# mLSTM with a bilinear feed-forward on one core: the weights' low words folded into the shifted high word, and the low part by one subtraction

## The chip, the cores and the metric

The kernel runs on one core of one Trainium2 chip. The core has a matrix engine (TensorE, PE in the profile, with its weight loads as PEld), a vector engine (VectorE, DVE), a scalar engine (ScalarE, ACT), GpSimd (POOL) and a queue engine that issues the DMAs (SyncE, SP). The metric is the time of one execution in device microseconds; lower is better.

## The reference

The inputs are q, k, v and an output gate (4 batches, 8 heads, 768 steps, 40 elements), an input and a forget gate per head and step, and three weight matrices. The first part is an mLSTM, written as a recurrence:

```
m_new = max(f[t] + m, i[t])
C = exp(f[t] + m - m_new) * C + exp(i[t] - m_new) * v[t] k[t]^T
n = exp(f[t] + m - m_new) * n + exp(i[t] - m_new) * k[t]
y[t] = sigmoid(o[t]) * (C q[t]) / max(|n . q[t]|, 1)
```

The second part takes y as x, 3072 tokens by 320, and computes `((x @ w_a) * (x @ w_b)) @ w_out` with w_a and w_b of 320 by 1536 and w_out of 1536 by 320. The weights are 64-bit floating-point numbers: the reference multiplies random numbers by a NumPy double and so gets doubles. The result is 32-bit.

## The kernel before

The recurrence is done in chunks of 128 steps: 6 chunks for each of 4 batches, 24 pieces of work, in the order of time and then of batch. A chunk is an attention inside the chunk (scores, decay factors, weighted sum) plus a product with the state C that the chunks before left. The feed-forward runs over nine blocks of two or three chunks (256 or 384 tokens); block kb is interleaved by hand with the attention of later chunks, by a counter in the outer loop (lines 912 to 928). For each of the 12 slices of 128 columns of w_a and w_b, `up` (line 685) makes two accumulators in PSUM, tag "pu" with three buffers; their product is split into a high and a low part, and `down` (line 664), two slices later, multiplies both with w_out into "pd".

Every operand of these products is held as two numbers of the reduced type fp32r, a high part h and a low part l with h + l close to the 32-bit value, and a product is made of three matmuls: h times h, h times l, l times h.

So the weights must first be turned from 64-bit words into an h and an l. That is `weights()`, lines 308 to 384. The weights come in 32 stages (`weight_stages`, line 276): per slice of 384 columns of w_a and w_b four stages of 128 rows, one stage with the 64 rows left of both, and three stages of 128 rows of w_out with 320 columns. `fetch(x)` issues the DMA of a stage's raw words on SP, four stages ahead. `first(x)` takes the words apart:

- L336, ScalarE: the high words, read as 32-bit numbers, are scaled by a Prelu into t, which lies in one of four shared tiles `step`. This makes the exponent fit.
- L343, VectorE: W is t's bits shifted left by three. W is the weight cut off to a 32-bit number, with the last three bits empty.
- L344, VectorE: t becomes W's sign and exponent bits alone.
- L346, VectorE: r is the low word as a whole number times 2^-52 times t, that is, what W lacks.

W and r take a buffer each of the pool tag "cv", which has eight. `second(x)`, called after `first(x + 1)`, makes the two parts:

- L359, ScalarE: h is W rounded to fp32r.
- L361 and L362, TensorE: two matmuls with the identity `eye[0]` and its negative `eye[1]` add r and -h in a PSUM tile pc, which takes one of the three "pu" buffers.
- L363, VectorE: l is pc + W.

h and l lie in the same memory as the raw words (tag s{x}), so L359 can't write before the last reader of the raw words is done. In the four stages with the 64 rows left, h and l go to tiles ct and then by four DMAs (L367, L368) to their place. The generator `weights()` is advanced by hand: at set points in the first attention chunks, and then every sixth step of the feed-forward. `need(x)` (line 303) advances it further where a matmul comes to use a stage. `issue_after` in these lines keeps an instruction behind a named one on its engine; apart from that the framework's scheduler sets the order of each engine's instructions, by priorities, from a simulation at compile time. It also places all waits and buffers.

The two identities of fp32r are made at the start from `ident` by two scalings on ScalarE (L65 to L67).

Of the kernel before, what the change touches and what calls it, by code (L numbers as in the profile page):

```python
# [8 lines left out]
F32 = mybir.dt.float32  # L9
BF16 = mybir.dt.bfloat16  # L10
F32R = mybir.dt.float32r
# [4 lines left out]
ALU = mybir.AluOpType  # L16
# [4 lines left out]
def kernel(  # L21
# [13 lines left out]
    nc = tc.nc  # L35
    B, H, S, D = q.shape
    DM, DFF = w_a.shape
    P = 128
# [5 lines left out]
    NTB = TB * P  # L44
    WCH = 384
    CVB = 8
# [6 lines left out]
    wpool = ctx.enter_context(tc.tile_pool(name="wpool", bufs=1))  # L53
# [4 lines left out]
    ps_up = ctx.enter_context(tc.tile_pool(name="ps_up", bufs=3, space=PSUM))  # L58
# [3 lines left out]

    ident = wpool.tile([P, P], F32, name="ident")
    make_identity(nc, ident)
    eye = [wpool.tile([P, P], F32R, name=f"eye{j}") for j in range(2)]  # L65
    for j in range(2):
        nc.scalar.mul(eye[j], ident, 1.0 - 2.0 * j)  # L67
    NQ = 2

    qk = [wpool.tile([P, 2, H, 64], F32, name=f"qk{j}") for j in range(NQ)]  # L70
# [20 lines left out]
    for j in range(3):  # L91
        r = slice(j * BH, (j + 1) * BH)
# [10 lines left out]
    x = ident[0:BH, 0:BH].rearrange("k (x j) -> k x j", j=2)  # L103
# [204 lines left out]
    def weights():  # L308
        stages = list(weight_stages())
        held = {}  # L310

        def fetch(x):
            if x < len(stages):
                src = stages[x]
                n = src[0].shape[1]
                raw = rpool.tile([P, n], I64, tag=f"s{x}", name=f"raw{x}")
                r0 = 0
                behind = [y for first, y in BEHIND if x >= first][-1]
                with tc.issue_after(issued[behind]), tc.issue_after(issued.get("w", issued[behind])):
                    for a in src:  # L320
                        raw_in = nc.sync.dma_start(raw[r0:r0 + a.shape[0]], a).ins
                        r0 += a.shape[0]
                issued["w"] = raw_in
                held[x] = [raw, n]

        def first(x):
            raw, n = held[x]
            W = cpool.tile([P, WCH], F32, tag="cv", name="cw", bufs=CVB)[:, :n]
            t = step[x % len(step)][:, :n]
            words = raw.bitcast(U32).rearrange("p (n w) -> p n w", w=2)  # L330
            lo, hi = words[:, :, 0], words[:, :, 1]
            wu, tu = W.bitcast(U32), t.bitcast(U32)


            with tc.issue_after(after["e", 0] if x > 2 else issued["k", 0]):
                nc.scalar.activation(  # L336
                    t, hi.bitcast(F32), AF.Prelu, scale=2.0 ** -112, alpha=-(2.0 ** 32)
                )

            step_of = (None, ("b", 0), ("b", 0), ("r", 0), ("r", 0))  # L340
            y = after[step_of[x] if x < len(step_of) and step_of[x] else ("r", 1)] if x > 0 else issued["k", 0]
            with tc.issue_after(y):
                nc.vector.tensor_scalar(wu, tu, 3, None, op0=ALU.logical_shift_left)  # L343
            nc.vector.tensor_scalar(tu, wu, 0xFF800000, None, op0=ALU.bitwise_and)  # L344
            r = cpool.tile([P, WCH], F32R, tag="cv", name="cr", bufs=CVB)[:, :n]
            nc.vector.scalar_tensor_tensor(r, lo, 2.0 ** -52, t, op0=ALU.mult, op1=ALU.mult)  # L346
            held[x] += [W, r]

        def second(x):

            ready[0] = x + 1
            raw, n, W, r = held.pop(x)
            w = ws[x] = rpool.tile([P, 2, n], F32R, tag=f"s{x}", name=f"w{x}")
            h, l = w[:, 0], w[:, 1]
            last = len(stages[x]) > 1
            if last:
                h, l = (cpool.tile([P, WCH], F32R, tag="ct", name="ct", bufs=2) for _ in range(2))
            with tc.issue_after(after["e", 0]):
                nc.scalar.copy(h, W)  # L359
            pc = ps_up.tile([P, NTB], F32, tag="pu", name=f"pc{x}")[:, :n]  # L360
            nc.tensor.matmul(pc, eye[0], r, start=True, stop=False)  # L361
            nc.tensor.matmul(pc, eye[1], h, start=False, stop=True)  # L362
            nc.vector.tensor_tensor(l, pc, W, op=ALU.add)  # L363
            if last:
                for j in range(2):
                    rows, other = (slice(64 * i, 64 * i + 64) for i in (j, 1 - j))
                    nc.sync.dma_start(w[rows, j].bitcast(F32), h[rows].bitcast(F32))  # L367
                    nc.sync.dma_start(w[other, j].bitcast(F32), l[rows].bitcast(F32))  # L368

        fetch(0)  # L370
        yield -1
        for x in range(1, 4):
            fetch(x)
        for x in range(len(stages) + 1):
            fetch(x + 4)
            if x < len(stages):
                first(x)
                yield x
            if x > 0:
                second(x - 1)  # L380
                yield x
        for x in qks2:
            for w in range(2):
                nc.gpsimd.memset(x[:, w, :, 3 * D:], 0.0)
# [527 lines left out]
    for kb in range(NB):  # L912
# [5 lines left out]
        for x, _ in enumerate(moe_block(kb)):  # L918
# [3 lines left out]
            while acc >= 1.0 and not done:  # L922
                acc -= 1.0
                r = next(att, ("done", 99))
# [34 lines left out]
```

## Time and profile before

| | |
|---|---|
| runs, median | 569.38 us (3 runs, 569.38 to 571.58) |
| profiled execution, span from first to last instruction | 572.6 us |
| TensorE matmuls | 551.1 us busy (96%), 4864 |
| VectorE | 429.3 us busy (75%), 992 |
| ScalarE | 215.4 us busy (38%), 526 |
| GpSimd | 130.2 us busy (23%), 182 |
| mean granted TensorE clock | 0.966 |
| data moved | 68.35 MB, 119 GB/s |

The profile is of one execution. Busy time of an engine counts the time in which at least one of its instructions runs. A matmul's end is modelled and matmuls overlap, so a group of matmuls has more busy time than it adds to the chain. The chain is followed back from the last instruction: at each step to whatever released it, or to the instruction before it on its engine. The granted clock is the share of full speed that TensorE was given. A row of a group has the line, engine, operation, out<-in by the program's names, shapes and count, then busy time and mean duration in ns, then the idle time of the engine before them and what ended it. No time of the profiled execution is given beside its span.

### The profile page before, as it was taken

What the parts mean: (1) busy time and instruction counts of PE and PEld (TensorE: products, weight loads), DVE (VectorE), ACT (ScalarE), POOL (GpSimd) and SP (SyncE); (2) the same over time, 40 slices, a digit from 0 to 9 for tenths busy, and PEclk for the clock granted to TensorE, in tenths of its full rate; (3) what the DMA queues carried; (4) which work ended last, traced back from release to release, by engine and by line L of the source; (5) the groups of instructions that cost most, each with busy time, mean ns of one, the idle gap of its engine ahead of it and who ended that gap; (6) DMA issues with size and microseconds to landing.
All of it is one profiled execution on the core that took longest, in us unless ns stands there. A gap on an engine that the chain in (4) does not pass through costs nothing.

```text
span 572.6 us, 12629 instructions
## 1 busy us (share of the span) xinstructions
PE 551.1 (96%) x4864; PEld 529.6 (92%) x4864; DVE 429.3 (75%) x992; ACT 215.4 (38%) x526; POOL 130.2 (23%) x182
## 2 busy tenths in 40 slices
PE   3999999989999998999999999999999999999997
PEld 2879999979999998999999999999999899999996
DVE  6888888598659979499759997699849864954342
ACT  3767357243234434144523334424413611411111
POOL 3132143164114313123303330322212200200000
PEclk9859997689999999999999999999999999999999
DMA  9999946247235974367854877466638503200000
GB/s 209 276 224 325 200 95 127 52 107 156 68 74 132 181 145 105 92 108 149 153 108 107 139 159 137 115 148 145 134 93 130 138 20 99 59 2 23 2 2 34
DMA packets 199864, 68.35 MB, mean 119 GB/s; under 512 B 184476, under 2 KB 193084, under 8 KB 199804
## 3 DMA queue, kind: packets, MB, share of 16 engines
q1 hardware_dynamic: 199804, 67.55, 54.9%
q8 instruction: 38, 0.62, 0.5%
q14 instruction: 22, 0.18, 0.1%
HBM read 41.11 MB, written 5.97 MB: 82 GB/s over the span
## 4 chain that ended last, share of the span: by engine, by line
PE 82%; DVE 6%; DMA 4%; ACT 3%; issue 2%; SPq 1%; POOL 0%; ACTq 0%; DVEq 0%; POOLq 0%
PE pu L702 44%; PE pd L673 20%; PE pV L512 3%; PE pU L536 3%; PE pS L460 2%; PE pX L609 2%; PE pS L775 1%; PE pV L824 1%; DMA osig<-in_o_gate_dram 1%; PE pI L486 1%; PE pc L361 1%; PE pI L793 1%; ACT gbc L405 1%; DMA T<-qks 1%; DMA qk<-in_k_dram 1%
## 5 line engine op out<-in xcount | busy, mean ns | idle before, releaser
L702 PE MATMUL pu<-xh,w 128*128 128x384 f32 (+1 forms) x1080 | 281.2, 327 | 0.7 <-ACT g L708 0.5
L702 PE MATMUL pu<-xl,w 128*128 128x384 f32 (+1 forms) x648 | 209.0, 324 | 0.0
L702 PEld LDWEIGHTS pu<-xh,w 128*128 128x128 f32 x1080 | 194.6, 193 | 3.7 <-ACT g L708 1.4
L673 PE MATMUL pd<-w,gh 128*128 128x320 f32 x576 | 128.8, 313 | 0.0
L702 PEld LDWEIGHTS pu<-xl,w 128*128 128x128 f32 x648 | 124.9, 193 | 0.1
L709 DVE TENSOR_TENSOR g<-pu,g 128x384 f32<-128x384 f32 (+1 forms) x108 | 54.7, 506 | 84.8 <-PE pu L702 44.1
L673 PEld LDWEIGHTS pd<-w,gh 128*128 128x128 f32 x576 | 97.4, 190 | 0.2
L673 PE MATMUL pd<-w,gl 128*128 128x320 f32 x288 | 86.4, 314 | 0.0
L708 ACT COPY g<-pu 128x384 f32<-128x384 f32 (+1 forms) x90 | 39.7, 442 | 120.2 <-PE pu L702 108.1
L405 ACT ACTIVATE gbc<-gbc,gtab 128x128 f32<-128x128 f32 x160 | 49.1, 389 | 18.8 <-POOL gbc L398 18.8
L673 PEld LDWEIGHTS pd<-w,gl 128*128 128x128 f32 x288 | 53.2, 189 | 0.1
L713 DVE TENSOR_TENSOR gl<-g,gh 128x384 fp32r<-128x384 f32 (+1 forms) x92 | 49.9, 543 | 2.1
L502 POOL TENSOR_TENSOR vw<-va,gtab 128x336 f32<-128x336 f32 x14 | 10.6, 760 | 160.2 <-PE pU L536 157.1
L711 DVE CAST gh<-g 128x384 fp32r<-128x384 f32 (+1 forms) x108 | 43.1, 399 | 1.9
L588 POOL TENSOR_TENSOR osig<-osig,den 128x320 f32<-128x320 f32 x24 | 20.3, 844 | 91.8 <-DVE den L583 60.1
L398 POOL TENSOR_SCALAR_AFFINE_SELECT gbc<-gbc 128x1024 f32<-128x1024 f32 x20 | 24.2, 1212 | 46.3 <-DMA va<-in_v_dram 33.3
L423 ACT CAST qks<-qk 128x320 bf16<-128x320 f32 x36 | 16.3, 453 | 38.3 <-DMA T<-qks 30.9
L469 DVE TENSOR_TENSOR gbc<-gbc,pb 128x512 f32<-128x512 f32 x36 | 25.0, 696 | 1.0 <-ACT pb L467 0.9
L512 PEld LDWEIGHTS <-pb 128*128 128x128 bf16 x576 | 23.4, 96 | 2.6 <-issue 0.9
L465 DVE TENSOR_TENSOR gbc<-pS,gbc 128x512 f32<-128x512 f32 x36 | 23.9, 679 | 1.9 <-PE pS L460 1.9
L512 PE MATMUL pV<-va,pb 128*128 128x42 bf16 x288 | 25.3, 182 | 0.0
L471 DVE TENSOR_TENSOR pb<-gbc 128x512 bf16<-128x512 f32 x36 | 25.0, 695 | 0.0
(133 smaller groups left out, 841.7 us busy)
## 6 DMA issues: line engine op xcount, KB each, us to landing
gbc<-g_dram SPq DMA_DIRECT2D x20, 512.0 KB
va<-in_v_dram SPq DMA_DIRECT2D x24, 160.0 KB
qk<-in_q_dram SPq DMA_DIRECT2D x24, 160.0 KB
qk<-in_k_dram SPq DMA_DIRECT2D x24, 160.0 KB
osig<-in_o_gate_dram SPq DMA_DIRECT2D x24, 160.0 KB
raw<-in_moe_w_out_dram SPq DMA_DIRECT2D x12, 320.0 KB
out_dram<-o SPq DMA_DIRECT2D x24, 160.0 KB
raw<-in_moe_w_a_dram SPq DMA_DIRECT2D x8, 384.0 KB
```

The source lines that it names most:

```text
L398: nc.gpsimd.affine_select(E, E, pattern=[[0, H], [1, P]], compare_op=ALU.is_ge, fill=-1e30, base=0, channel_multiplier=-1,)
L405: nc.scalar.activation(E[:, h], E[:, h], AF.Exp, bias=beta[:, h:h + 1])
L465: nc.vector.tensor_tensor(E, pS, E, op=ALU.mult)
L469: nc.vector.tensor_tensor(E, E, pb[:, 0], op=ALU.subtract)
L471: nc.vector.tensor_tensor(pb[:, 1], E, mid, op=ALU.subtract)
L512: nc.tensor.matmul(pv[:, h], pb[i][:, h % HH, :], vb[j][:, h], start=(x == 0), stop=(x == len(terms) - 1),)
L673: nc.tensor.matmul(pd[t][:, 0:DM], a[:, cols], w, start=(ff == 0 and first), stop=(ff == NF - 1 and last),)
L702: nc.tensor.matmul(acc[j], a, r, start=(x == 0), stop=(x == len(terms) - 1),)
L708: (nc.vector.tensor_copy if ff in [1, 2] else nc.scalar.copy)(g, acc[0])
L709: nc.vector.tensor_tensor(g, acc[1], g, op=ALU.mult)
L711: nc.vector.tensor_copy(gh, g)
L713: (nc.gpsimd if kb * 12 + ff < 16 else nc.vector).tensor_tensor(gl, g, gh.bitcast(F32), op=ALU.subtract)
```

## The change

The two identities go. The conversion keeps its Prelu, its W and its h. Of the low word only the top three bits are used: it is scaled by 2^-29 as a number, cut at 7 and written as a whole number into W's buffer; then one instruction shifts t left by three and puts these three bits under it. W then has all its bits filled, r is not made, and l is W - h, by one VectorE subtraction that reads both from SBUF. The part of the weight below W's last bit is no longer in h + l.

```diff
     make_identity(nc, ident)
-    eye = [wpool.tile([P, P], F32R, name=f"eye{j}") for j in range(2)]
-    for j in range(2):
-        nc.scalar.mul(eye[j], ident, 1.0 - 2.0 * j)
...
             with tc.issue_after(y):
-                nc.vector.tensor_scalar(wu, tu, 3, None, op0=ALU.logical_shift_left)
-            nc.vector.tensor_scalar(tu, wu, 0xFF800000, None, op0=ALU.bitwise_and)
-            r = cpool.tile([P, WCH], F32R, tag="cv", name="cr", bufs=CVB)[:, :n]
-            nc.vector.scalar_tensor_tensor(r, lo, 2.0 ** -52, t, op0=ALU.mult, op1=ALU.mult)
-            held[x] += [W, r]
+                nc.vector.tensor_scalar(wu, lo, 2.0 ** -29, 7.0, op0=ALU.mult, op1=ALU.min)
+            nc.vector.scalar_tensor_tensor(
+                wu, tu, 3, wu, op0=ALU.logical_shift_left, op1=ALU.bitwise_or
+            )
+            held[x] += [W]
...
-            raw, n, W, r = held.pop(x)
+            raw, n, W = held.pop(x)
...
             with tc.issue_after(after["e", 0]):
                 nc.scalar.copy(h, W)
-            pc = ps_up.tile([P, NTB], F32, tag="pu", name=f"pc{x}")[:, :n]
-            nc.tensor.matmul(pc, eye[0], r, start=True, stop=False)
-            nc.tensor.matmul(pc, eye[1], h, start=False, stop=True)
-            nc.vector.tensor_tensor(l, pc, W, op=ALU.add)
+            nc.vector.tensor_tensor(l, W, h.bitcast(F32), op=ALU.subtract)
```

## The prediction

> **What bounds the kernel now.** I read first the page's busy lines, its forty slices and the chain that ended last.
>
> ```profile
> PE 551.1 (96%) x4864; PEld 529.6 (92%) x4864; DVE 429.3 (75%) x992; ACT 215.4 (38%) x526; POOL 130.2 (23%) x182
> ...
> PE   3999999989999998999999999999999999999997
> ...
> PEclk9859997689999999999999999999999999999999
> DMA  9999946247235974367854877466638503200000
> ...
> PE 82%; DVE 6%; DMA 4%; ACT 3%; issue 2%; SPq 1%; POOL 0%; ACTq 0%; DVEq 0%; POOLq 0%
> PE pu L702 44%; PE pd L673 20%; PE pV L512 3%; PE pU L536 3%; PE pS L460 2%; PE pX L609 2%; PE pS L775 1%; PE pV L824 1%; DMA osig<-in_o_gate_dram 1%; PE pI L486 1%; PE pc L361 1%; PE pI L793 1%; ACT gbc L405 1%; DMA T<-qks 1%; DMA qk<-in_k
> ```
>
> TensorE works nearly without a gap: 551.1 of 572.6 us busy, and 82% of the chain is its own matmuls. A matmul taken off it is time saved wherever the chain runs through it. Two things qualify that: the granted clock falls to half in some early slices, and the DMA queues are full in the first five slices, which are where the weights come in. So I cut the span into stretches by the clock. The columns are the window, its length, each engine's busy time (instructions), the granted clock, the DMA share and GB/s.
>
> ```profile
> 20.00:25.00 5.00, 4.71 (x42) 3.81 (x41) 4.71 (x14) 3.60 (x5) 0.14 (x1) 1.00 1.01 316
> 25.00:42.00 17.00, 16.09 (x90) 13.47 (x89) 14.19 (x37) 10.48 (x26) 5.00 (x7) 0.50 1.04 241
> 42.00:93.00 51.00, 50.95 (x435) 47.00 (x434) 42.77 (x112) 29.30 (x72) 13.37 (x19) 1.00 0.83 201
> 93.00:111.00 18.00, 18.00 (x81) 17.52 (x82) 10.66 (x25) 8.92 (x23) 5.11 (x7) 0.53 0.32 58
> 111.00:125.00 14.00, 11.47 (x65) 10.08 (x64) 13.93 (x33) 5.12 (x16) 7.42 (x13) 0.88 0.41 94
> 125.00:573.00 448.00, 439.02 (x4076) 427.76 (x4075) 329.06 (x745) 149.23 (x370) 93.76 (x117) 1.00 0.49 103
> ```
>
> All conversion of weights lies before 125 us. There TensorE is full from 42 to 111 us while VectorE has slack (42.77 of 51.00, then 10.66 of 18.00). From 111 to 125 it turns round: VectorE 13.93 of 14.00, TensorE 11.47. After 125 us the change touches nothing directly. The grouped lines give what the change edits:
>
> ```profile
> L346 DVE SCALAR_TENSOR_TENSOR cr<-raw,qks 128x384 fp32r<-128x384 uint32 (+1 forms) x32 | 18.4, 575 | 0.2
> ...
> L363 DVE TENSOR_TENSOR w<-pc,cw 128x384 fp32r<-128x384 f32 (+1 forms) x28 | 14.4, 521 | 4.9 <-PE pc L362 4.8
> ...
> L361 PE MATMUL pc<-cr,eye 128*128 128x384 f32 (+1 forms) x32 | 13.7, 427 | 0.9 <-DVE cr L346 0.9
> L344 DVE TENSOR_SCALAR qks<-cw 128x384 uint32<-128x384 uint32 (+1 forms) x32 | 13.4, 419 | 0.2
> L343 DVE TENSOR_SCALAR cw<-qks 128x384 uint32<-128x384 uint32 (+1 forms) x32 | 13.4, 418 | 2.1 <-PE pc L361 1.9 <-ACT qks L336 0.2
> ...
> L362 PE MATMUL pc<-w,eye 128*128 128x384 f32 (+1 forms) x28 | 10.9, 390 | 1.4 <-ACT w L359 1.1
> ...
> L363 DVE TENSOR_TENSOR ct<-pc,cw 128x384 fp32r<-128x384 f32 x4 | 2.2, 547 | 0.0
> ...
> L362 PE MATMUL pc<-ct,eye 128*128 128x384 f32 x4 | 1.5, 382 | 0.0
> ```
>
> There are 32 conversions, 20 with 384 columns and 12 with 320. Each has four VectorE steps and two identity products.
>
> **The change part by part.**
>
> *The identity products go* (64 matmuls with their weight loads). Their busy times overlap their neighbours', so the price is what the chain charges. Here is the chain by line, first in the window 0 to 110, then 110 to 150 us:
>
> ```profile
> by line: PE pu L702 19.5%; PE pS L775 7.6%; PE pV L824 7.1%; PE pU L536 6.7%; PE pd L673 6.0%; PE pc L361 4.8%; PE pI L793 4.8%; PE pc L362 3.8%; issue 3.7%; PE pT L762 3.7%; PE pX L609 3.0%; DMA g_i<-in_i_gate_dram 2.9%; PE pE L739 2.5%; P
> ```
> ```profile
> by line: PE pu L702 48.0%; PE pd L673 19.3%; DMA gbc<-g_dram 9.5%; ACT gbc L405 5.5%; POOL gbc L398 2.8%; PE pV L512 2.3%; PE pU L536 2.1%; issue 1.8%; ACT g L708 1.6%; ACT o L682 1.5%; PE pc L361 1.1%; PE pc L362 1.1%; PE pI L486 1.0%; PE
> ```
>
> L361 and L362 have 4.8% and 3.8% of 110 us, 9.5 us, and 1.1% twice of 40 us, 0.9 us: 10.3 us together. A second way, from steady rows near the end of the chain (start, length, pieces):
>
> ```profile
> 557.66 2.80 PE pu L702 x16
> 560.46 1.31 PE pd L673 x9
> ```
>
> Sixteen matmuls of 384 columns in 2.80 us are 0.175 us each, nine of 320 in 1.31 us 0.146 us each; 40 x 0.175 + 24 x 0.146 = 10.5 us at full clock. Products in the half-clock windows cost double and others lie where another engine ends last, so the two ways may agree. I take 10.3 us. The bounds are 0 (all of it is swallowed by another limit, a rival below) and 10.3 plus the waits of the next part.
>
> *The waits on the products go.* Waiting engine and line, releaser, total us, times, longest:
>
> ```profile
> DVE w L363 <- PE pc L362: 4.8, 5, 2.5
> ...
> DVE cw L343 <- PE pc L361: 1.9, 4, 0.6
> ...
> PE pc L362 <- ACT w L359: 1.1, 1, 1.1
> ...
> PE pc L361 <- DVE cr L346: 0.9, 1, 0.9
> ```
>
> TensorE waited 1.1 + 0.9 us inside the products themselves. Both are in the stretch 111 to 125 us, where the chain runs through a load of gates, its mask on GpSimd and its exponentials on ScalarE (the 9.5%, 2.8% and 5.5% of the second chain row); what is late next is that, so I count nothing and keep 0 to -2.0 us for the range. VectorE's 4.8 + 1.9 us are slack given to an engine that mostly has some.
>
> *VectorE's steps.* Before, the sum of the five VectorE rows is 13.4 + 13.4 + 18.4 + 14.4 + 2.2 = 61.8 us. After, the two single-tensor steps and the product become one single-tensor step (scale and minimum, on every second word) and one two-tensor step (shift and or). No row shows exactly the first: it lies between L344 (one tensor, dense, 13.4 us for 32) and L346 (reads the same alternate words, 18.4); I take 15.9, the middle, since it has the form of the one and the operand of the other. The shift and or is priced like L346, two tensors from SBUF, 18.4. The last subtraction now reads W and h from SBUF instead of PSUM and SBUF: 16.6 as now, or 18.4 if it behaves like L346. In all 48.4 to 55.2 us, so VectorE gains 6.6 to 13.4 us. That is off the path except where the chain runs through VectorE, around 83 to 90 us:
>
> ```profile
> by line: DMA w<-ct 15.8%; PE pu L702 10.4%; DVE w L363 8.3%; PE pI L793 8.1%; DVE qks L344 7.7%; PE pd L673 7.3%; issue 5.8%; DVE cw L343 5.7%; DVE cr L346 5.7%; DVE T L765 4.3%; DVE cst L543 4.0%; DVE xl L614 3.4%; DVE ct L363 3.3%; DVE nu
> ```
>
> The three lines that shrink have 7.7 + 5.7 + 5.7 = 19.1% of 14 us, 2.7 us. Their total goes from 13.4 + 13.4 + 18.4 = 45.2 to 31.8 to 36.8 us, so 19 to 30% of the 2.7 us goes, 0.5 to 0.8 us; I take 0.6. Per conversion that is 0.26 to 0.42 us, and TensorE loses a pair of products there, 0.35 us; neither is left clearly behind, so the 0.6 us counts.
>
> *A price against the change: GpSimd.* Durations in ns, least, median, greatest, of the product and of the subtraction:
>
> ```profile
> L346 DVE SCALAR_TENSOR_TENSOR cr<-raw,qks x32: 475/548/1227, 12.3 to 118.8; 128x384 fp32r<-128x384 uint32 x20, 128x320 fp32r<-128x320 uint32 x12
> ```
> ```profile
> L363 DVE TENSOR_TENSOR w<-pc,cw x28: 476/542/558, 21.7 to 122.9; 128x384 fp32r<-128x384 f32 x16, 128x320 fp32r<-128x320 f32 x12
> ```
>
> L346 with two SBUF operands is stretched to 1227 ns at its worst, L363 with one PSUM operand never above 558. At their usual lengths L346 would be 20 x 548 + 12 x 475 ns = 16.7 us instead of 18.4, so this costs 1.7 us over 32. The subtraction moves from the second kind to the first: up to 1.8 us more on VectorE, contained above, hidden by the 6.6 us at least that VectorE wins. If that cover were gone it would cost those 1.8 us. The Trainium skill has this as a rule (SBUF — State Buffer, section Who interferes with whom): a VectorE instruction with two SBUF inputs contends with a GpSimd instruction that reads SBUF, and one with a single SBUF input outside the two-port modes doesn't. The two rows bear it out; by the rule the subtraction is 18.4, by the row of today 16.6, and the time is the same.
>
> *Two scalings at the start go* with `eye`. They ran while ScalarE had nothing else to do, and are worth nothing. But the first function table was loaded for them:
>
> ```profile
> 0.73 1.28 ACT L67 ACT_TABLE_LOAD   x1 [0.73 <-PEq L943]
> 2.16 0.51 ACT L67 ACTIVATE eye<-ident 128x128 fp32r<-128x128 f32 x2
> 9.29 0.30 ACT L205 COPY g_tab<-g_m 32x128 f32<-32x128 f32 x1 [6.62 <-DVE g_m L198]
> ```
>
> The load now falls to the next ScalarE instruction, the copy at 9.29 us on which the first transposes' copies hang. If it ran only after that copy's wait it would cost its 1.28 us; at 0.73 it ran ahead of its own user's operand, which I take again: 0, with +1.3 us kept as a bound.
>
> *Buffers and order.* The pool of eight "cv" buffers now serves one tile per conversion and not two, and PSUM's three "pu" buffers lose 32 users to the up products. Both can only let work start sooner. The step tile t has its last reader one step after the Prelu and not three. No DMA, no SP or GpSimd queue entry is added or moved. VectorE's new first step waits only for the raw words, no longer for ScalarE's Prelu; what is queued behind it waits less. The compiler orders every engine's instructions anew, which no row prices. The idle time of TensorE after 125 us, 448.00 - 439.02 = 9.0 us, is the most that a luckier order could win there; a less lucky one costs like amounts. I take 0.
>
> *Sum.* -10.3 - 0.6 = -10.9 us. Against the profiled execution's span that is 572.6 - 10.9 = 561.7 us. The span lies 3.2 us above the median of the runs, 569.38, and no row splits that difference; nothing of it is touched, so the median becomes 558.5 us.
>
> **The rivals.**
>
> *A. DMA sets the pace before 70 us.* With the queues full, conversions can't come sooner and only what lies later pays. The chain from 70 to 110 us:
>
> ```profile
> by line: PE pu L702 32.5%; PE pI L793 13.1%; PE pd L673 9.4%; PE pV L824 6.4%; DMA w<-ct 5.5%; PE pc L361 4.5%; PE pU L536 2.9%; DVE w L363 2.9%; PE pS L775 2.7%; DVE qks L344 2.7%; PE pc L362 2.6%; PE pX L609 2.4%; issue 2.0%; DVE cw L343
> ```
>
> 4.5 + 2.6% of 40 us is 2.8 us, with the 0.9 after 110 us 3.7: 565.7 us. For it speaks the DMA share of 1.01 and 1.04 from 20 to 42 us. Against it speaks how long the words lie before use:
>
> ```profile
> 7.75 0.73 SPq L321 DMA_DIRECT2D raw<-in_moe_w_b_dram  x1
> ...
> 34.61 1.16 SPq L321 DMA_DIRECT2D raw<-in_moe_w_out_dram  x2
> ```
> ```profile
> 12.33 0.56 ACT L336 ACTIVATE qks<-raw 128x384 f32<-128x384 f32 x1 [0.91 <-DMA raw<-in_moe_w_b_dram]
> ...
> 46.58 0.50 ACT L336 ACTIVATE qks<-raw 128x320 f32<-128x320 f32 x1
> ```
>
> The second stage's words, issued at 7.75 us, were waited for until 12.33, so landing took 4.6 us in a full queue. The fifteenth's, issued at 34.61, were first read at 46.58 us: 12.0 - 4.6 = 7.4 us to spare, more than what the chain saves up to there. Chance 0.10.
>
> *B. One half-clock stretch less.* Clock 0.50 from 25 to 42 us and 0.53 from 93 to 111. If one of these 17 us stretches goes, its work takes half: -10.9 - 8.5 gives 550.0 us. Chance 0.12.
>
> *C. One half-clock stretch more.* The products are dense, full-array work: 64 of the 713 matmuls in the five rows from 20 to 125 us. If another stretch follows from their absence, -10.9 + 8.5 gives 567.0 us, no change. Chance 0.14.
>
> *D. Slower: the clock stays down.* The same, deciding when the half clock lasts more than 22 us longer than now (each such us loses half of itself, against 10.9): its place is 42 to 93 us, now at full clock between the two stretches. Two further stretches of 17 us give -10.9 + 17 = +6.1, 575.5 us; the whole gap, +14.6, gives 584.0 us. For it: the low clock is near. Against it: in 42 to 93 us the products are few among the 435 matmuls, and the rest is as dense as after 125 us, at clock 1.00. Chance 0.08.
>
> On B to D the Trainium skill (TensorE: Matmul & The Clock Gate, section Part 1: The HAM clock gate) says that the clock halves after an idle window of about 3.4 us and returns after a busy one. By that rule removing work from a TensorE that stays busy changes no clock, and the time is the forecast. The trace agrees only in the size of the clock's two steps: from 93 to 111 us TensorE is busy 18.00 of 18.00 at 0.53, so I leave chances on both sides.
>
> *E. The steps aren't what the diff says* (another compiled form, a converted copy added): no saving, 569.4 us. All parts are single instructions of kinds that the kernel has. Chance 0.03.
>
> **How the numbers follow.** The forecast has the rest, 0.53, about 555 to 562 us: the 2.0 us of waits and some luck in the order below, 1.3 us of the table load and a few us of new waits above. What a measurement of this kernel can tell from no change is about 0.5%, 2.8 us: faster means under 566.5. Faster: forecast 0.53, A 0.07 (its 565.7 lies close to the edge), B 0.12 and of C 0.04 where the added stretch is shorter, 0.76. Same: the rest of A and C, 0.13, with E 0.16. Slower: D, 0.08. The range reaches from B, 550, to just above C, 568; left out are D, half of B and E, under 2 in 10.
>
> **What would show it.** Right: no matmul on an identity tile in the conversions, some 4800 TensorE instructions; VectorE's three lines at 48 to 55 us in all, the subtraction sometimes stretched beyond 600 ns where GpSimd works; the last conversion about 10 us sooner than now; the time after the last conversion as long as now. Wrong: a TensorE that waits for raw words before 70 us (A), half-clock windows of another total than the 35 us of now (B to D), a table load behind a wait at 9 us, or idle TensorE after 125 us well above 9.0 us, which would mean that the new order gave the gain back.

## The result, and the profile after

The changed kernel takes 572.12 us (median, 570.13 to 576.28, 14 runs) where the kernel before takes 569.27 us (566.94 to 571.58, 14 runs). The ratio is 1.0056, 95% interval 1.0037 to 1.0075: slower by 0.56%, a small loss but clear of the noise. The forecast was 558.5 us, the range 550 to 568. Ratios leave out single runs over 1.5% above the fastest of their kernel; e4 and e11 below have one and two such runs, and without them their medians are 560.15 and 571.04 us instead of 560.76 and 571.64.

The profiled execution has a span of 568.7 us and took 571.18 us, close to the median. That of before had a span of 572.6 us, so the two profiles alone would say 3.9 us faster. The clock explains that. Mean granted TensorE clock over the runs: 0.980 for before (three later sessions, medians 0.979 to 0.9805), but 0.966 in its one profiled execution; 0.9665 for after, 0.967 in its profile. Within the runs of before, 0.01 of clock goes with 3.5 to 4.9 us, so the profiled execution of before lies 5 to 7 us above what its usual clock gives. So the medians decide, and the profiles are read for where the time lies.

The page of the changed kernel, with busy lines, the forty slices of TensorE and of its clock, and the chain:

```profile
PE 534.9 (94%) x4800; PEld 514.8 (91%) x4800; DVE 418.3 (74%) x960; ACT 213.4 (38%) x524; POOL 133.2 (23%) x182
...
PE   3858999999999899999899999999999999999997
...
PEclk9857799999999999999999999999999999999999
...
PE 71%; DMA 9%; DVE 7%; issue 3%; ACT 2%; SPq 2%; POOL 1%; ACTq 0%; DVEq 0%; POOLq 0%
PE pu L696 40%; PE pd L667 18%; PE pV L506 3%; PE pU L530 2%; PE pS L454 2%; DMA raw<-in_moe_w_out_dram 2%; PE pX L603 1%; DMA T<-qks 1%; DMA osig<-in_o_gate_dram 1%; PE pV L818 1%; PE pI L480 1%; DMA raw<-in_moe_w_a_dram 1%; DMA va<-in_v_d
```

TensorE has 16.2 us less to do (534.9 after 551.1) and 64 matmuls fewer, as the diff says. But the gap between busy time and span grew from 21.5 to 33.8 us, the chain has 71% of TensorE where it had 82%, DMA has 9% where it had 4, and two lines of raw weight words are now in it. The clock is low (8 or less) in the slices 2 to 5, where before it was low in 2, 3 and 7 to 9: as much in all in these two executions (mean 0.967 and 0.966), so what the change does to the clock shows only in the medians over the runs.

The same stretches as in the prediction, with the same columns (the first numbers after the length are TensorE, its weight loads, VectorE, ScalarE and GpSimd; the last three the clock, the DMA share and GB/s):

```profile
20.00:25.00 5.00, 2.66 (x25) 2.14 (x24) 4.90 (x12) 4.42 (x7) 0.31 (x1) 0.80 1.03 320
25.00:42.00 17.00, 10.76 (x74) 9.08 (x73) 16.94 (x42) 11.30 (x29) 5.55 (x6) 0.50 0.98 239
42.00:93.00 51.00, 46.48 (x359) 43.95 (x360) 40.72 (x100) 27.20 (x68) 13.60 (x20) 0.85 0.74 181
93.00:111.00 18.00, 18.00 (x144) 17.63 (x144) 10.31 (x23) 8.46 (x20) 7.54 (x10) 1.00 0.43 80
111.00:125.00 14.00, 14.00 (x114) 12.94 (x113) 7.57 (x19) 4.58 (x12) 5.41 (x7) 1.00 0.51 131
125.00:573.00 448.00, 432.15 (x3999) 419.52 (x3997) 324.35 (x739) 149.27 (x375) 95.58 (x117) 0.99 0.50 103
```

Three things changed places. From 20 to 42 us TensorE is idle for 8.6 of 22 us (1.2 before) while VectorE is full, 4.90 of 5.00 and 16.94 of 17.00. From 42 to 93 us TensorE is idle for 4.5 us at a clock of 0.85 (0.05 us at 1.00 before). After that it is full at full clock where before it had the second half-clock stretch and the gap at 111 to 125 us.

The edited lines of VectorE among the groups of the changed kernel (the shift and or, the subtraction, the scaling; us in all, mean ns, idle time before them):

```profile
L341 DVE SCALAR_TENSOR_TENSOR cw<-qks,cw 128x384 uint32<-128x384 uint32 (+1 forms) x32 | 17.4, 557 | 0.2 <-ACT qks L333 0.2
...
L357 DVE TENSOR_TENSOR w<-cw,w 128x384 fp32r<-128x384 f32 (+1 forms) x28 | 16.7, 599 | 0.0
...
L340 DVE TENSOR_SCALAR cw<-raw 128x384 uint32<-128x384 uint32 (+1 forms) x32 | 12.7, 419 | 2.4 <-DMA raw<-in_moe_w_out_dram 2.3
```
The first step of all conversions in the changed kernel, by its line (ns least/median/greatest, then the first and last start in us):

```profile
L340 DVE TENSOR_SCALAR cw<-raw x32: 276/345/898, 10.3 to 72.6; 128x384 uint32<-128x384 uint32 x20, 128x320 uint32<-128x320 uint32 x12
```

The same in the kernel before:

```profile
L343 DVE TENSOR_SCALAR cw<-qks x32: 309/353/1032, 11.0 to 116.9; 128x384 uint32<-128x384 uint32 x20, 128x320 uint32<-128x320 uint32 x12
```

The lines sum to 12.7 + 17.4 + 16.7 us, and with 2.2 us for the four subtractions into ct (a mean of 551 ns) to 49.0 us, within the forecast 48.4 to 55.2. The conversions begin as before, but the last starts at 72.6 us and not at 116.9: 44 us sooner, where the prediction had "about 10 us". They were not made faster by that much; they were moved ahead of other work. VectorE's timeline of the changed kernel at 30 us shows it (start, length, line, what, count):

```profile
30.42 0.20 DVE L577 RECIPROCAL den<-den 128x8 f32<-128x8 f32 x1
30.54 2.93 DVE L340 TENSOR_SCALAR cw<-raw 128x320 uint32<-128x320 uint32 x7
33.40 0.48 DVE L341 SCALAR_TENSOR_TENSOR cw<-qks,cw 128x320 uint32<-128x320 uint32 x1
33.80 0.34 DVE L340 TENSOR_SCALAR cw<-raw 128x384 uint32<-128x384 uint32 x1
34.07 0.88 DVE L341 SCALAR_TENSOR_TENSOR cw<-qks,cw 128x320 uint32<-128x320 uint32 x2
34.87 0.47 DVE L583 TENSOR_TENSOR osig<-pV,osig 128x320 f32<-128x320 f32 x1
```

And that of the kernel before at the same place:

```profile
30.46 0.20 DVE L583 RECIPROCAL den<-den 128x8 f32<-128x8 f32 x1
30.58 0.56 DVE L346 SCALAR_TENSOR_TENSOR cr<-raw,qks 128x384 fp32r<-128x384 uint32 x1
31.05 0.84 DVE L343 TENSOR_SCALAR cw<-qks 128x320 uint32<-128x320 uint32 x1
31.93 0.75 DVE L344 TENSOR_SCALAR qks<-cw 128x320 uint32<-128x320 uint32 x1
32.61 0.48 DVE L589 TENSOR_TENSOR osig<-pV,osig 128x320 f32<-128x320 f32 x1
```

After the reciprocal at 30.4 us the second chunk's gating product (osig, L583, before L589) is the attention's next step on VectorE. Before, three conversion steps lie ahead of it and it starts at 32.61 us. After, seven first steps stand in a row, 2.93 us, then four more steps, and it starts at 34.87. The product that it waits for, on GpSimd, ended at 31.42 us after and at 31.72 before:

```profile
30.70 0.72 POOL L582 TENSOR_TENSOR osig<-osig,den 128x320 f32<-128x320 f32 x1 [3.21 <-DVE den L577]
```
```profile
30.74 0.98 POOL L588 TENSOR_TENSOR osig<-osig,den 128x320 f32<-128x320 f32 x1 [1.27 <-DVE den L583]
```

So from there on only the steps ahead of it on VectorE held it back, 3.4 us after and 0.9 us before. In the compiled order of VectorE's instructions, 21 conversions are finished ahead of the first cast of the feed-forward's product (gh); before there are 9. That cast, from which on the products with w_out can begin, starts 7.4 us later, at 57.7 us (after) and not at 50.3 (before):

```profile
L705 DVE CAST gh<-g x108: 278/353/1241, 57.7 to 561.6; 128x384 fp32r<-128x384 f32 x72, 128x256 fp32r<-128x256 f32 x36
```
```profile
L711 DVE CAST gh<-g x108: 278/352/1245, 50.3 to 565.3; 128x384 fp32r<-128x384 f32 x72, 128x256 fp32r<-128x256 f32 x36
```

Who waits for that, in the changed kernel (engine, line, releaser, us, times, longest):

```profile
PE pU L530 <- POOL vw L802: 4.6, 4, 1.7
ACT qks L333 <- DMA raw<-in_moe_w_out_dram: 4.6, 5, 2.0
...
PE pS L769 <- DVE T L759: 3.2, 2, 2.1
...
DVE cw L340 <- DMA raw<-in_moe_w_out_dram: 2.3, 2, 1.2
```

TensorE waits for operands of the attention: 4.6 us for vw, which GpSimd makes, and 3.2 us for the transposed T that VectorE copies. Before, it did not wait for this copy, and less for vw:

```profile
PE pU L536 <- POOL vw L808: 0.9, 1, 0.9
```

Conversions now also run into their DMA: the later words are waited for (4.6 and 2.3 us), which is rival A's wait, brought about by conversions that come too early and not by ones that are needed. In the chain of the changed kernel (followed back from 130 us) two loads of words stand end to end (start, length, what):

```profile
36.62 5.52 DMA raw<-in_moe_w_a_dram
...
42.17 9.66 DMA raw<-in_moe_w_out_dram
...
51.85 0.04 DVE cw L340
```

### The profile page after: what moved, and what is told of

The parts are those of the page before. It is cut to its first block, busy times and chain, and to the rows that moved or that the text cites. A ratio compares the mean times of both kernels' runs of the same rounds, so it can differ in the third digit from the quotient of the medians.

```text
span 568.7 us, 12439 instructions
## 1 busy us (share of the span) xinstructions
PE 534.9 (94%) x4800; PEld 514.8 (91%) x4800; DVE 418.3 (74%) x960; ACT 213.4 (38%) x524; POOL 133.2 (23%) x182
## 3 DMA queue, kind: packets, MB, share of 16 engines
q1 hardware_dynamic: 199804, 67.55, 55.2%
## 4 chain that ended last, share of the span: by engine, by line
PE 71%; DMA 9%; DVE 7%; issue 3%; ACT 2%; SPq 2%; POOL 1%; ACTq 0%; DVEq 0%; POOLq 0%
PE pu L696 40%; PE pd L667 18%; PE pV L506 3%; PE pU L530 2%; PE pS L454 2%; DMA raw<-in_moe_w_out_dram 2%; PE pX L603 1%; DMA T<-qks 1%; DMA osig<-in_o_gate_dram 1%; PE pV L818 1%; PE pI L480 1%; DMA raw<-in_moe_w_a_dram 1%; DMA va<-in_v_dram 1%; PE pS L769 1%; SPq L162 1%
## 5 line engine op out<-in xcount | busy, mean ns | idle before, releaser
L707 DVE TENSOR_TENSOR gl<-g,gh 128x384 fp32r<-128x384 f32 (+1 forms) x92 | 52.3, 570 | 1.9
L417 ACT CAST qks<-qk 128x320 bf16<-128x320 f32 x36 | 16.3, 453 | 36.6 <-DMA T<-qks 30.4
L530 PEld LDWEIGHTS pU<-vw,qk 128*64 128x64 f32 x320 | 18.4, 152 | 8.1 <-POOL vw L802 5.5
L421 DVE TENSOR_TENSOR r<-qk,qks 128x320 f32<-128x320 f32 x36 | 19.7, 546 | 8.1 <-ACT qks L417 8.1
L530 PE MATMUL pU<-vw,qk 128*64 128x42 f32 x320 | 21.2, 248 | 4.6 <-POOL vw L802 4.6
```

The source lines that it names most:

```text
L421: (nc.gpsimd if 2 * n + j < 4 else nc.vector).tensor_tensor(r, src[:, j], ph, op=ALU.subtract)
L530: nc.tensor.matmul(pu[r:r + 64, x], nat(n)[0][:, 1, h, :], s["vw"][:, h], start=True, stop=True)
L707: (nc.gpsimd if kb * 12 + ff < 16 else nc.vector).tensor_tensor(gl, g, gh.bitcast(F32), op=ALU.subtract)
```

## The experiments

The theory after the result: **crowding**. W and r took a buffer "cv" each, so eight buffers held four conversions, and a conversion's last step waited in TensorE's queue for its products. With one buffer for a conversion and no product, the scheduler sends up to eight conversions ahead on VectorE, ahead of the first chunks' attention; TensorE idles and its clock stays low longer. The rivals: the **products** held the clock up as dense work (C and D of the prediction); the **low word's new steps** cost more than they show. This theory is the "brake theory" of the expectations: the products' wait was the brake.

All ratios are to the kernel before in the same session: e1 to e4 in one, e5 to e8 in a second, e9 to e11 in a third, on another chip. Where a diff leaves lines out there are three dots; in e1 and e5 these lines also make the two identities, each times -0.5.

**e1: products kept.** The new W, but two products with half the negative identity make pc, and l is pc + W.

```diff
...
-            nc.vector.tensor_tensor(l, W, h.bitcast(F32), op=ALU.subtract)
...
+            nc.tensor.matmul(pc, eye[0], h, start=True, stop=False)
+            nc.tensor.matmul(pc, eye[1], h, start=False, stop=True)
+            nc.vector.tensor_tensor(l, pc, W, op=ALU.add)
```

> The changed kernel with the two identity products put back as they cost before: both multiply h by -0.5 times an identity into PSUM, and the subtraction adds that to W; the new VectorE steps stay. Brake theory (the products, late in TensorE's queue, had held the conversions back; without them 21 conversions instead of 9 stand ahead of the first cast of the first up slice in VectorE's order, and the attention of the first two chunks waits): the order of before comes back (9 there), the early idle time of TensorE goes, and the time is about that of before or up to 1% under it, 564 to 570 us, although TensorE has 10 us more to do than in the changed kernel. Rival, the clock or the new steps cost what was lost: the time is the changed kernel's 572 plus the products' 10, 578 to 583 us.

576.47 us (12 runs), ratio 1.0113 [1.0078, 1.0147], clock 0.9725. Neither expectation came: it lies above the theory's 564 to 570 us and below the rival's 578 to 583. The order is back, with 9 conversions ahead of the first gh, at 51.8 us, but the time of before is not. So the products' wait does hold the conversions back; that putting it back repairs the time isn't shown.

**e2: products gone only.** The kernel before with its four VectorE steps, without identities and products; l is W - h. r is still made and takes its buffer, but nobody reads it, so the low word's part is left out.

```diff
...
-            nc.vector.tensor_tensor(l, pc, W, op=ALU.add)
+            nc.vector.tensor_tensor(l, W, h.bitcast(F32), op=ALU.subtract)
```

> The kernel before with only the products gone: its four steps on VectorE stay, r is made and read by nobody (so the bits below W's last are left out of the weights, and W's last three bits stay empty), and l is W minus h from SBUF. Brake theory: conversions run ahead here too (13 of 32 ahead of the first cast of an up slice, before 9), VectorE has 7 us more to do than in the changed kernel, and the gain of 10 us is lost in part or whole: 566 to 573 us. Rival, only the new first step (which needs no Prelu) or the freed buffers let the conversions run ahead: this kernel keeps both as before and gains the products' 10 us, 557 to 561 us.

565.12 us (6 runs), 0.9895 [0.9841, 0.9949], clock 0.9755. This lies between the two expectations. Taking the products out is a gain by itself, some 6 of their 10 us, at a clock little below that of before. The same step from e1 to the changed kernel, 576.47 to 572.12, gains 0.6% by the ratios. The new W in place of the old four steps, with less work, loses: 565.12 to 572.12. Two things differ beside the work: in e2 eight buffers hold four conversions, and the first step of each waits for ScalarE's Prelu. e10 below tells them apart.

**e3: paced.** In the changed kernel, each conversion's first step is also kept behind the newest cast gh on VectorE.

```diff
-            with tc.issue_after(y):
+            ghs = issued.get("gh", [])
+            z = ghs[-1] if len(ghs) >= 1 else y
+            with tc.issue_after(y), tc.issue_after(z):
...
-            nc.vector.tensor_copy(gh, g)
+            issued.setdefault("gh", []).append(nc.vector.tensor_copy(gh, g).ins)
```

> The changed kernel with one more order: a conversion's first VectorE step stands behind the newest cast of an up slice (gh) that the program has traced by then; nothing is computed otherwise. VectorE's order then has 10 conversions ahead of the first such cast and 17 ahead of the fifth (before 9 and 15; changed kernel 21 and 32). Brake theory: the gain that was forecast comes, 557 to 562 us. Rival, late words from memory: conversions that wait longer can't wait for words, so this comes out the same as the brake theory; rival, clock: the time stays within 1% of the changed kernel, 568 to 576 us.

577.97 us (6 runs), 1.012 [1.0077, 1.0164], clock 0.9585. This is above all that was expected, 557 to 562 by the theory and 568 to 576 by the rival. Its waits show a miss in the other direction:

```profile
PE pu L698 <- DMA w<-ct: 6.6, 3, 4.5
```

Now TensorE waits 6.6 us for the weights themselves. Fewer conversions ahead isn't better without limit.

**e4: two buffers.** The changed kernel with two buffers, so that no more than two conversions are under way.

```diff
-    CVB = 8
+    CVB = 2
```

> The changed kernel with two buffers for W instead of eight, which keeps the conversions from being more than two apart: 15 conversions stand ahead of the first cast of an up slice. Brake theory: between the changed and the paced kernel, 562 to 569 us. If the eight buffers, free for twice as many conversions as before, were the whole cause: 557 to 562 us. Rival, clock: 568 to 576 us.

560.76 us (6 runs), 0.9827 [0.9772, 0.9882], clock 0.980. One constant turns the loss into most of the gain that was forecast, as was expected if the eight buffers were the whole cause. The stretches of e4:

```profile
20.00:25.00 5.00, 3.22 (x35) 2.86 (x34) 4.94 (x11) 4.73 (x7) 0.51 (x1) 1.00 1.01 308
25.00:42.00 17.00, 12.37 (x77) 10.13 (x78) 16.38 (x41) 10.89 (x26) 4.14 (x6) 0.53 0.99 248
42.00:93.00 51.00, 49.18 (x406) 46.20 (x405) 45.83 (x111) 30.48 (x80) 15.46 (x24) 0.96 0.79 187
```

From 42 to 93 us the clock is 0.96 where it was 0.85, and TensorE has done 406 matmuls where it had done 359. From 20 to 42 us it is still idle for 6.4 us (8.6 in the changed kernel, 1.2 before) beside a VectorE that is nearly full, so most of that early idle time is not due to the eight buffers. TensorE's wait for vw is 2.6 us here; the wait for VectorE's copy of T is gone. VectorE at the same place:

```profile
30.54 0.20 DVE L577 RECIPROCAL den<-den 128x8 f32<-128x8 f32 x1
30.66 1.07 DVE L340 TENSOR_SCALAR cw<-raw 128x320 uint32<-128x320 uint32 x2
31.65 1.43 DVE L341 SCALAR_TENSOR_TENSOR cw<-qks,cw 128x320 uint32<-128x320 uint32 x2
33.01 0.48 DVE L583 TENSOR_TENSOR osig<-pV,osig 128x320 f32<-128x320 f32 x1
```

Two first steps and not seven, and the gating product at 33.01 us, 1.9 us sooner. The first cast gh starts at 50.0 us with 15 conversions ahead of it, and the last first step at 86.2 us.

**e5: ballast.** The changed kernel, with two products of h put back that nobody reads, so that they cost TensorE their work but no conversion waits for them.

```diff
...
+            nc.tensor.matmul(pc, eye[0], h, start=True, stop=False)
+            nc.tensor.matmul(pc, eye[1], h, start=False, stop=True)
             nc.vector.tensor_tensor(l, W, h.bitcast(F32), op=ALU.subtract)
```

> The changed kernel with the two identity products put back as work that nobody reads: h times -0.5 times an identity, twice, into PSUM; the subtraction stays W minus h from SBUF. VectorE's order is that of the changed kernel (21 conversions ahead of the first cast of an up slice), TensorE has its 10 us back. Theory, the conversions running ahead make TensorE wait and by that keep its clock down: clock as in the changed kernel, 0.963 to 0.970, and 576 to 583 us, slower than the changed kernel by the products. Rival, the products are dense work that holds the clock up: clock back at 0.978 to 0.983, the half clock's 5 to 8 us come back and the time is 572 to 576 us.

572.95 us (12 runs), 1.0065 [1.0030, 1.0101], clock 0.9755. Against the changed kernel's 572.1 the products are nearly free, and the clock is higher by 0.009. The theory's 576 to 583 us at an unchanged clock did not come. Here dense work went with a higher clock, as the rival has it, though not with its 0.978 to 0.983; e11 asks whether it does so in the better order. TensorE's idle time between 20 and 93 us is 6.8 us in e5's profile, where the changed kernel has 13.1: part of what the products need was idle time there.

**e6: control.** The kernel before with four buffers, which hold two conversions.

```diff
-    CVB = 8
+    CVB = 4
```

> The kernel before with four buffers for W and r instead of eight, a control: its conversions are held two apart by the buffers, as in the run with two buffers for W, but its order on VectorE stays nearly the same (8 conversions ahead of the first cast of an up slice, was 9), since the products hold them back anyway. Theory: within 0.7% of before, 566 to 574 us. Rival, fewer buffers are good for any version of this kernel, and the gain of the run with two buffers has nothing to do with the change: 558 to 563 us.

576.92 us (6 runs), 1.0131 [1.0081, 1.0182], clock 0.972. More than the 566 to 574 us expected, and the rival's 558 to 563 is out: fewer buffers are no gift to any version. Where products already hold the conversions back, they cost 1.3%.

**e7: two apart by order.** Eight buffers, but the first step of stage x is kept behind the subtraction of stage x - 2.

```diff
-            with tc.issue_after(y):
+            with tc.issue_after(y), tc.issue_after(issued.get(("l", x - 2), y)):
```

> The changed kernel with all eight buffers, and a conversion's first VectorE step ordered behind the last step of the conversion two before it. VectorE's order is nearly that of the run with two buffers (15 conversions ahead of the first cast of an up slice; 19 steps ahead of the second chunk's output gate, 26 in the changed kernel). Theory, the distance is what counts: as with two buffers, 558 to 565 us, clock 0.975 or more. Rival, the buffers themselves or chance: 568 us or more.

560.76 us (6 runs), 0.9841 [0.9801, 0.9881], clock 0.979. The same as e4 with all the buffers there: it is the order on VectorE, not the memory.

**e8: behind the gate.** Conversions from the sixth stage on are kept behind the second chunk's gating product, and are free after it.

```diff
-            y = after[step_of[x] if x < len(step_of) and step_of[x] else ("r", 1)] if x > 0 else issued["k", 0]
+            y = after[step_of[x] if x < len(step_of) and step_of[x] else ("o", 1)] if x > 0 else issued["k", 0]
...
-        nc.vector.tensor_tensor(yv, num[:, :, 0:D], yv, op=ALU.mult)
+        after["o", n] = nc.vector.tensor_tensor(yv, num[:, :, 0:D], yv, op=ALU.mult).ins
```

> The changed kernel with all conversions from the sixth on ordered, on VectorE, behind the second chunk's output gate instead of behind its reciprocal: 15 conversion steps stand ahead of it instead of 26, and later the order is that of the changed kernel (20 conversions ahead of the first cast of an up slice, all 32 before the fifth). Theory, what stood ahead of the first two chunks' attention is the larger part of the lost time: 564 to 569 us. Rival, the crowding after them (25 to 75 us) is the larger part: 569 to 573 us.

575.17 us (10 runs), 1.0083 [1.0047, 1.0119], clock 0.961. Slower than both expectations, 564 to 569 and 569 to 573 us. Once free, the conversions crowd the next chunks; from the waits of e8:

```profile
PE pU L530 <- POOL vw L802: 9.2, 3, 6.8
```

TensorE waits 9.2 us for vw, more than the changed kernel's 4.6, and the first cast gh starts at 62.0 us. A single gate only moves the crowd.

**e9 and e10: three and four buffers.** The changed kernel with three buffers and with four. e9:

```diff
-    CVB = 8
+    CVB = 3
```

> The changed kernel with three buffers W instead of eight. VectorE's order has 17 finished conversions ahead of the first cast gh (15 with two buffers, 18 with four, 21 with eight). Theory 'the number of conversions queued ahead of attention sets the loss': between 560.8 (two) and 572.1 (eight) by that count, 560.8 + 11.3 x 2/6 = about 564.6 us. Rival 'two apart is a special place, any more loses it all': 570 to 572. Rival 'all that matters is that there are fewer than eight': about 561.

561.10 us (6 runs), 0.9809 [0.9763, 0.9854], clock 0.9785. e10:

```diff
-    CVB = 8
+    CVB = 4
```

> The changed kernel with four buffers W. Theory 'the number queued ahead sets the loss', 18 conversions ahead of the first cast gh: 560.8 + 11.3 x 3/6 = about 566.5 us. Rival 'two apart is a special place': 570 to 572. Rival 'fewer than eight is enough': about 561.

564.74 us (6 runs), 0.9881 [0.9834, 0.9928], clock 0.973. With two, three, four and eight conversions under way the kernel takes 560.8, 561.1, 564.7 and 572.1 us. Two is no special place, and the count of conversions ahead of the first gh is too simple a measure: it gave 564.6 for three. Four buffers give e2's time, 565.1, and e2 also holds four conversions: the old first step, with its wait for the Prelu, isn't needed to explain e2. The start of the first gh orders these kernels better: with two buffers, two by order, three, four, eight, and behind the gate it is 50.0, 50.1, 50.4, 52.5, 57.7 and 62.0 us in their profiles, for 560.8, 560.8, 561.1, 564.7, 572.1 and 575.2 us.

**e11: ballast at two buffers.** e5 with two buffers:

```diff
-    CVB = 8
+    CVB = 2
```

> Two buffers W, and two products of h with a scaled identity put back behind the cast h, whose result nobody reads (so the low part doesn't wait for them). With eight buffers the same products cost 0.9 us (573.0 beside 572.1) at a clock higher by 0.009. Theory 'the products cost their own work, and only where the clock is low anyway do they give it back': with two buffers the clock is already 0.980, so they cost their 10 us or nearly, 568 to 571 us at a clock of 0.98. Rival 'the products are free beside the start of the kernel whatever the order': about 561. Rival 'dense work raises the clock here too': 564 to 567 at a clock of 0.985 or more.

571.64 us (12 runs), 1.0014 [0.9978, 1.0051], clock 0.9785. Against e4 the two products cost 10.9 us (10.6 us by the two ratios, 1.0014 and 0.9827, uncertain by some 4 us) at nearly the same clock. That agrees with the forecast's term of 10.3 us, and with the first of the three expectations. It also shows that the crowd's price depends on what else TensorE has to do: from eight buffers to two is worth 13 us without the ballast (1.0056 to 0.9827), but only 3 us with it (1.0065 to 1.0014, as large as its uncertainty). The stretches of e11:

```profile
25.00:42.00 17.00, 15.01 (x89) 12.56 (x88) 15.78 (x38) 11.05 (x28) 5.30 (x7) 0.50 0.97 256
42.00:93.00 51.00, 50.39 (x370) 45.09 (x370) 43.16 (x104) 28.71 (x75) 13.22 (x19) 0.91 0.77 180
93.00:111.00 18.00, 18.00 (x143) 17.04 (x141) 9.75 (x23) 5.66 (x10) 6.33 (x9) 1.00 0.49 94
111.00:125.00 14.00, 14.00 (x107) 12.71 (x106) 3.74 (x10) 6.11 (x16) 5.42 (x7) 1.00 0.38 87
```

The products fill TensorE (50.39 of 51.00 us from 42 to 93) and the clock there is 0.91, below e4's 0.96. In these two executions dense work did not hold the clock up.

**One account for all.** If a half clock costs a full TensorE half of its time, a run loses (1 - mean clock) x time. (From 93 to 111 us, full in both profiles, TensorE did 81 matmuls at a clock of 0.53 before and 144 at 1.00 after.) From the median times and clocks of the runs that the ratios use:

| kernel | us | clock | lost to the clock | the rest |
|---|---|---|---|---|
| before | 569.3 | 0.980 | 11.4 | 557.9 |
| after, eight conversions under way | 572.1 | 0.9665 | 19.2 | 552.9 |
| e10, four | 564.7 | 0.973 | 15.2 | 549.5 |
| e9, three | 561.1 | 0.9785 | 12.1 | 549.0 |
| e4, two | 560.2 | 0.980 | 11.2 | 549.0 |
| e7, two by order | 560.8 | 0.979 | 11.8 | 549.0 |
| e2, no products, old steps | 565.1 | 0.9755 | 13.8 | 551.3 |
| e3, paced | 578.0 | 0.9585 | 24.0 | 554.0 |
| e8, behind the gate | 575.2 | 0.961 | 22.4 | 552.8 |
| e1, products kept | 576.5 | 0.9725 | 15.9 | 560.6 |
| e6, before with four buffers | 576.9 | 0.972 | 16.2 | 560.7 |
| e5, after with ballast | 573.0 | 0.9755 | 14.0 | 559.0 |
| e11, two with ballast | 571.0 | 0.9785 | 12.3 | 558.7 |

Kernels with products have a rest of 558 to 561 us, those without, in a good order, 549 to 551: the products' price. The changed kernel gains 5.0 us in the rest, 8.9 (557.9 to some 549.0) less 3.9, and gives 7.8 back to the clock: +2.8 us. The 3.9 are of the size of TensorE's added idle time: between 20 and 93 us it is 13.1 us in the changed kernel's profile and 8.2 in e4's. The rule prices 0.01 of clock at 5.7 us, where within the runs of before it went with 3.5 to 4.9; the split between the two losses is uncertain by that much.

## Why the prediction was wrong

**The step that failed** is "Buffers and order": "Both can only let work start sooner" and "The compiler orders every engine's instructions anew ... I take 0." The first sentence is true of each conversion and false of the kernel: on VectorE, work that starts sooner stands ahead of something else, as the gating product shows that was ready at 31.42 us and started at 34.87. Eight buffers for eight conversions in place of four, without the products' wait, put 21 finished conversions ahead of the feed-forward's first cast in place of 9. This cost about 11 us (12 to 13 by the ratios), as e4 and e7 show, which only bound how far the conversions run ahead (15 in place of 21): 572.1 to 560.8. The bound given, luck within the 9.0 us of idle time after 125 us, looked at the wrong place. There it is now 568.7 - 125 - 432.15 = 11.6 us, little more; the order did its harm before 93 us.

**The products, -10.3 us: right, where the order is good.** e11 against e4 gives 10.9, uncertain by some 4. In the changed kernel's own order the same products cost only 0.9 us (e5): there the term and the order aren't two separate sums.

**The waits on the products, 0 to -2.0 us, and VectorE's -0.6 us:** VectorE's sum came within its bounds (49.0 us), in part by luck: the new first step took 12.7 us, under its 13.4 to 18.4, and the subtraction 18.9 with its four into ct, over its 16.6 to 18.4. What that gain was worth in the changed kernel isn't shown. The waits of VectorE on pc (4.8 + 1.9 us) were called slack; they also held the conversions back, as e1 and e5 show, which differ in whether the subtraction waits for the products and reads them: 9 and 21 conversions ahead of the first gh. But e1 is not the faster of the two, so a brake by itself did not help. The ratios of e4 and e7, 0.9827 and 0.9841, are 9.1 to 9.8 us of 569.27; against the forecast sum of 10.9 the terms were right to some 2 us, once the crowd is gone. The rival of costly new steps falls with them, since both have these steps.

**GpSimd: right.** The subtraction went to a mean of 599 ns. Its median is 544; 2.3 us of the 16.7 are stretch (16 x 544 + 12 x 477 ns is 14.4). One case in the changed kernel, first VectorE's timeline:

```profile
53.97 1.42 DVE L357 TENSOR_TENSOR w<-cw,w 128x384 fp32r<-128x384 f32 x1
```

and GpSimd's:

```profile
53.88 1.09 POOL L392 TENSOR_SCALAR_AFFINE_SELECT gbc<-gbc 128x1024 f32<-128x1024 f32 x1 [8.78 <-DMA gbc<-g_dram]
54.94 0.80 POOL L549 TENSOR_TENSOR cr<-cst,cb 128x168 f32<-128x168 f32 x1
```

1.42 us in place of 0.55, while GpSimd works from 53.88 to 55.74 us. The rule of the Trainium skill (SBUF — State Buffer, section Who interferes with whom), that a VectorE instruction with two SBUF inputs contends with a GpSimd instruction that reads SBUF, agrees with it: the same line's greatest was 558 ns when one operand came from PSUM. It was priced at up to 1.8 us, and at 2.3 did not decide.

**The table load: right at 0.** It stayed at 0.73 us.

**The median from the profile.** The 3.2 us between span and median were carried over as they stood. They were no fixed offset: that execution had a clock of 0.966 where 0.980 is usual. The half clock of about 35 us in it, read as the kernel's own, is 2 x 11.4 = 23 us at the usual clock.

**The rivals.** The change loses 7.8 us to the clock, about the 8.5 of C, but comes out slower, as only D had it. Its cause is another than C named. e4, e7 and e9 have no products and a clock of 0.979 to 0.980, as before has; e11 has products and the same. Only with a crowded VectorE did the products go with a higher clock (e5, by 0.009). D had its place right, 42 to 93 us at 0.85, and was given 0.08 because what is left there is "as dense as after 125 us", which no longer held when TensorE waited. A appeared as a wait but is no cause: in e4 the same words come by the same queue, and the longest wait of a conversion for them is 0.6 us.

**What stays open.** Whether the idle time makes the low clock, or both follow from sparse work in the first chunks, isn't told apart: in the profiles of e4 and e2 (mean clock 0.980 and 0.985) TensorE idles 5.7 us each between 25 and 50 us, in that of the changed kernel (0.967) 6.5 us. Between 50 and 75 us it is 0.7 and 0.2 us against 3.1, which goes with the clock in these three, but the kernel before lost clock from 93 to 111 us without any idle time. Nor is it settled why e1 and e6 are slow: with products, their first gh starts at 51.8 and 49.6 us, about as before, yet their clock is 0.972 and their rest 3 us above that of before. The split of the crowd's price between idle time and clock is an estimate.

## What to carry to other kernels

A wait that looks like slack on an engine with time to spare can be what keeps prefetched work from running ahead in its queue. When a change takes such a wait away or frees buffers, count how many pieces of the prefetched work can now run ahead on the in-order engine and what stands behind them, and bound them, by the number of buffers or by an explicit order: here two or three were worth 2% against eight, while pacing too tightly (e3) came out slower than eight. And before a profile is subtracted from, compare its mean clock with that of the other runs.

## What the runs showed of the hardware

The half clock comes in pieces. In the trace's records of the granted clock, the low stretches of the changed kernel are 23.89, 6.83, 3.41 and 3.41 us long, those of e4 17.07 and 3.41 us before the end: whole multiples of 3.41 us. The Trainium skill (TensorE: Matmul & The Clock Gate, section Part 1: The HAM clock gate) states a window of 3413 ns, and the records agree with it. Its rule that the clock falls after an idle window isn't the whole of it here: in the profile of before, by the modelled ends of its matmuls, TensorE was busy for 50.95 of 51.00 us from 42 to 93 us, the clock fell to half between 93 and 94, and TensorE was then busy for 18.00 of 18.00 us at a mean of 0.53. The same program differs from run to run in its mean clock, and its time follows: in one session before had 566.77 us at 0.983 and 574.46 us at 0.970.
